# Six rotating weight blocks, wide products for a and b, and large stores on the hardware rings of ACT and SyncE, in a one-core attention-decode backward kernel

## The chip, the cores and the metric

One core of one Trainium2 chip runs the kernel. The metric is the device time of one execution in microseconds. The kernel before took 408.96 us in the median of three runs (407.39 to 410.54). Every profile shows one execution.

## What is computed

Forward and backward of a gated mix of two branches, for one token (D = 640), all in bf16: an attention decode over a cache of 4096 keys with 32 heads of 128, and a dense layer with the mish activation (F = 1728). The outputs are the mixed output and the gradients for x, K, V, wq, wo, w1, b1, w2 and the gate.

```python
q = (x @ wq).reshape(1, 1, 32, 128)
p = softmax(q . k_cache * 128**-0.5)        # 32 heads, 4096 keys each
a = (p . v_cache).reshape(1, 1, 4096) @ wo
h = x @ w1 + b1;  b = (h * tanh(softplus(h))) @ w2
g = sigmoid((x * gate_w).sum())
out = g * a + (1 - g) * b
# and the vjp of out for grad_out: dx, dK, dV, dwq, dwo, dw1, db1, dw2, dgate
```

K and V are 33.6 MB each and are read once; dK and dV have the same size and are written once. wq and wo (5.2 MB each) and w1 and w2 (2.2 MB each) are read, and as many bytes of gradients are written.

## The kernel before, in words

The 32 heads are taken in NP = 16 pairs, so the main loop has iterations i = 0 to 15, each with 16 slots s (`slot(i, s)`, L734). One pair's K or V is a tile of 128 partitions by 8192 elements (2 MB), a row of 16 KB per partition. Seven such buffers (`bufs`, tiles kv) go round. Slots 0 to 7 of iteration i transpose V of pair i for dP, slots 8 to 15 transpose K of pair i+1 for the next scores: TensorE transposes (L372), ACT copies the result out of PSUM (L375), TensorE multiplies two chunks later (L382). The softmax steps (`soft_max` to `soft_p`), `o_post`, `d_sum` and `ds_make` have fixed slots. VectorE writes dV and dK over V and K in the same buffer, in four outer products each (`outer`, L463): dV in slots 9, 10, 12 and 13, dK of the pair in slot 15 and in slots 0, 1 and 3 of the next iteration.

When a buffer's gradient is complete, `store_kv` (L725) issues its store, puts the buffer at the end of `free_q`, and `pump()` issues the next load in program order on SyncE. That load waits for the store to land. Stores are issued by GpSimd (software ring) while loads are left to issue, and by SyncE afterwards. V's store stands in slot 13, K's in slot 3 of the next iteration.

The heads fall into NG = 4 groups g of four pairs. Each group needs 1024 columns of wq (for q), a block of wo of 128 x 8 x 640 (for do, a and dwo), and leaves dwq and dwo in the same places. Before, all of wq is one resident tile `wqa`, in which w2 borrows the columns of groups 2 and 3 until dw2 is stored; wo has two buffers `wob`, group g in g mod 2. `do_sum` (L288) multiplies wo with da on VectorE, in eight rows; `dwo_row` (L353) writes dwo over wo on ACT. `dx_sum` (L484) multiplies wq with dq on VectorE, `dwq_row` (L350, in the helper `scaled`) writes dwq over wq on ACT. `mlp_dact` (L578) and `mlp_dw2` (L583) do the same with w2, `mlp_dxb` with w1, which holds buffer 4 until dw1 is stored.

What happens beside the attention is put into slots by hand: `plan(i, {s: [...]})` and `at(i, s, f, ...)` append work to slot (i, s). Each engine runs its instructions in this order; semaphores hold the dependencies. Before, wo of group g+2 is loaded one slot after group g's dwo store, into the same buffer. The work after the loop ends the last pair, and three small rows are stored by GpSimd at the end.

Of the kernel before, what the change touches and what calls it, by code (L numbers as in the profile page):

```python
# [17 lines left out]
def kernel(  # L18
# [54 lines left out]
    HC = 2 * GC  # L73
    R3 = 3 * D
# [31 lines left out]
    assert R3 <= HC and FN <= 3 * RC and FK % 3 == 1  # L106
    bufs = [big.tile([P, bufw.get(i, KVW)], BF16, name=f"kv{i}", tag=f"kv{i}") for i in range(NBUF)]
    wqa = big.tile([P, RC, H * Dh], BF16, name="wq", tag="wq")
    wob = [big.tile([P, 8, D], BF16, name=f"wo{i}", tag=f"wo{i}") for i in range(2)]
# [26 lines left out]
    def ld_w1():  # L136
# [4 lines left out]

    w2_pieces = ((wqa[:, 0:RC - 1, HC:HC + R3],
                  lambda v: v[0:FM, :].rearrange("(p k) n -> p (k n)", k=FK)[:, 0:(FK - 1) * D].rearrange(
                      "p (f x) -> p f x", x=R3)),
                 (wqa[:, RC - 1, HC:HC + D],
                  lambda v: v[0:FM, :].rearrange("(p k) n -> p (k n)", k=FK)[:, (FK - 1) * D:FK * D]),
                 (wqa[0:FR, RC - 1, HC + D:HC + 2 * D], lambda v: v[FM:F, :]))

# [4 lines left out]
    def ld_wq(c0, c1, eng=nc.sync):  # L153
        eng.dma_start(wqa[:, :, c0:c1], wq_v[:, :, c0:c1])

    def ld_wo(g):
        nc.sync.dma_start(wob[g % 2][:], wo_v[g])

    loads.append(ld_kv(kbuf, 0, Kv[0], 2, lambda: (ld_wq(0, GC), ld_wo(0))))
    loads.append(ld_kv(vbuf, 0, Vv[0], 1))  # L160
    loads.append((False, ld_w2))
    for i in range(1, NP):
        if i == 3:
            loads.append((False, lambda: ld_wq(GC, HC)))
            loads.append((False, lambda: ld_wo(1)))
        loads.append(ld_kv(kbuf, i, Kv[i], 1))
        loads.append(ld_kv(vbuf, i, Vv[i], 1))
        if i == 1:
            loads.append((True, ld_w1))
# [102 lines left out]
    def q_half(g, a, bank=misc):  # L272
        ps = bank([P, 2, 2, P], F32, "q_ps")
        for rc in range(RC):
            nc.tensor.matmul(ps[:].rearrange("p a h d -> p (a h d)"), lhsT=xc[:, rc:rc + 1].to_broadcast([P, P]),
                             rhs=wqa[:, rc, g * GC + a * 512:g * GC + (a + 1) * 512], start=(rc == 0), stop=(rc == RC - 1))
        for hh in range(2):
            h = slice(64 * hh, 64 * hh + 64)
            nc.scalar.copy(Qr[g % 2][h, 2 * a:2 * a + 2, :], ps[h, :, hh, :])
# [7 lines left out]
    def do_sum(g, k):  # L287
        nc.vector.scalar_tensor_tensor(junk[:], in0=wob[g % 2][:, k, :], scalar=1.0, in1=da_bc[:],  # L288
                                       op0=ALU.mult, op1=ALU.mult, accum_out=do8[g % 2][:, k:k + 1])
# [41 lines left out]
    def a_cols(g, c0=0, c1=RC):  # L331
        if c0 == 0:
            mst["a"] = misc([P, RC], F32, "a_ps")
        ps = mst["a"]
        wv = wob[g % 2][:].rearrange("p k (n c) -> p k c n", c=RC)
        for c in range(c0, c1):
            for k in range(8):
                nc.tensor.matmul(ps[:, c:c + 1], lhsT=wv[:, k, c, :], rhs=o8[:, k:k + 1],  # L338
                                 start=(k == 0), stop=(k == 7))
        if c1 == RC:  # L340
            if g == 0:
                nc.vector.tensor_copy(a_acc[:], ps[:])
            else:
                nc.vector.tensor_tensor(a_acc[:], a_acc[:], ps[:], ALU.add)
# [7 lines left out]
    def dwo_row(g, k):  # L352
        nc.scalar.mul(wob[g % 2][:, k, :], da_bc[:], o8f[:, k:k + 1])  # L353

    def st_dwo(g, eng, k0=0, k1=8):
        eng.dma_start(dwo_v[g][:, k0:k1], wob[g % 2][:, k0:k1])
# [125 lines left out]
    def dx_sum(g, part, c0, c1, rc):  # L482
        w = wqa[:, rc, g * GC + c0:g * GC + c1]
        nc.vector.scalar_tensor_tensor(w, in0=w, scalar=1.0, in1=dqrow[g % 2][:, c0:c1], op0=ALU.mult, op1=ALU.mult,  # L484
                                       accum_out=dq_acc[:, rc, part:part + 1])

    def dwq_row(g, c0, c1, rc, eng=nc.scalar):
        scaled(eng, wqa[:, rc, g * GC + c0:g * GC + c1], dqrow[g % 2][:, c0:c1], xf[:, rc:rc + 1])

    def st_dwq(c0, c1, eng):  # L490
        eng.dma_start(dwq_v[:, :, c0:c1], wqa[:, :, c0:c1])
# [74 lines left out]
    def mlp_b(c0, c1):  # L566
        if c0 == 0:
            mst["b"] = misc([P, RC], F32, "b_ps")
        for c in range(c0, c1):
            for k in range(FN):  # L570
                n, ks = frange(k)
                nc.tensor.matmul(mst["b"][:, c:c + 1], lhsT=w2row(k).rearrange("p (n c) -> p c n", c=RC)[:, c, :], rhs=act_b[0:n, ks], start=(k == 0), stop=(k == FN - 1))
        if c1 == RC:
            nc.vector.tensor_copy(b_acc[:], mst["b"][:])
# [6 lines left out]
    def mlp_dw2(k):  # L581
        n, ks = frange(k)
        nc.scalar.mul(w2row(k), db_bc[0:n, :], act_f[0:n, ks])  # L583

    def st_dw2():
        for t, v in w2_pieces:
            nc.gpsimd.dma_start(v(out_8), t)
# [21 lines left out]
    def st_dw1():  # L609
        nc.gpsimd.dma_start(dw1_v, bufs[mbuf["w1"]][:, 0:RC * F])  # L610
        free_q.append(mbuf["w1"])
        pump()
# [42 lines left out]
    for k in range(FN):  # L655
        at(*((2, 3), (2, 4), (2, 6), (2, 7), (2, 9), (2, 10), (2, 12), (2, 13), (2, 14), (3, 1), (3, 2), (3, 3), (3, 4),
             (3, 6))[k], mlp_dw2, k)
# [5 lines left out]
    plan(3, {9: [(st_dw2,)]})  # L663
    plan(4, {0: [(dh_row, 1)], 1: [(o_rows, 0)]})
    plan(4, {3: [(a_cols, 0, 0, 2)], 4: [(a_cols, 0, 2, 4)], 5: [(a_cols, 0, 4, 5)]})
    for k in range(8):
        at(4, (6, 7, 8, 9, 10, 12, 13, 14)[k], dwo_row, 0, k)
    plan(4, {5: rows(mlp_dxb, 0), 7: rows(mlp_dxb, 1), 14: rows(mlp_dxb, 2)})
    plan(5, {0: [(st_dwo, 0, nc.gpsimd)], 1: [(ld_wo, 2)], 5: rows(mlp_dxb, 3), 7: rows(mlp_dxb, 4), 14: dx(0, 0, 0, GC, 0)})
    plan(4, {10: [(ld_wq, HC, 2 * HC, nc.scalar)]})  # L670
    plan(6, {0: [(st_dw1,)]})

    for g in range(NG - 1):
        i = 4 * g + 4
        if g:
# [4 lines left out]
            plan(i + 1, {0: [(st_dwo, g, nc.gpsimd)]})  # L680
            if g + 2 < NG:
                plan(i + 1, {1: [(ld_wo, g + 2)]})
# [11 lines left out]
    plan(12, {8: [(st_dwq, 0, HC, nc.scalar)]})  # L694
    plan(14, {6: [(st_dwq, HC, HC + GC, nc.gpsimd)]})
# [6 lines left out]
    at(i + 1, 3, st_dwq, g * GC, g * GC + CA, nc.gpsimd)  # L702
# [31 lines left out]
    def slot(i, s):  # L734
# [16 lines left out]
        if chain_on:  # L751
            if s == 0:
                dq_row(i - 1)
            if s in (0, 1, 3):
                dk_quarter(i - 1, (0, 1, 3).index(s) + 1)
            if s == 3:
                store_kv(kbuf, i - 1, dKv[i - 1], nc.gpsimd if loads else nc.sync)
            if s == 2:
                soft_max(i)
            if s == 4:  # L760
                soft_maxt(i)
            if s == 7:
                soft_z(i)
# [9 lines left out]
        if s in (9, 10, 12, 13):  # L773
            outer(vbuf[i], st[i]["p"], Dr[(i // 4) % 2][:, i % 4, :], (9, 10, 12, 13).index(s))
            if s == 13:
                store_kv(vbuf, i, dVv[i], nc.gpsimd if loads else nc.sync)
# [118 lines left out]
    st_dwq(g * GC + CA, (g + 1) * GC, nc.gpsimd)  # L895
# [61 lines left out]
```

## Time and profile before

| | before |
|---|---|
| median of 3 runs | 408.96 us |
| span of the profiled execution | 405.7 us |
| bytes moved by DMA, mean rate | 164.88 MB, 406 GB/s |
| busy: PE / PEld / DVE / ACT / POOL | 299.9 / 275.3 / 279.1 / 259.9 / 25.1 us |
| DVE waiting for wo at L288 | 32.5 us in two waits, the longest 20.2 us |
| stores of K and V: issue to landing, median | 19.1 us (GpSimd, 25 stores), 25.5 us (SyncE, 5 whole stores) |
| loads of K and V: issue to landing, median | 18.9 us and 18.8 us |
| mean granted TensorE clock | 0.878 |

The profiled execution lasted 405.7 us from its first to its last instruction, 3.3 us less than the median of the runs. Times within it are counted from its start. PE is TensorE's matmuls, PEld its weight loads, DVE is VectorE, POOL is GpSimd, SP is SyncE. "Busy" leaves out DMA issues of the sequencers. A line such as "DVE junk L288 <- DMA wo: 32.5, 2, 20.2" reads: VectorE, at line 288, waited for the DMA that fills wo, 32.5 us in all, in 2 waits, the longest 20.2 us. In the tables by stage each engine's busy us and instruction count are followed by the granted clock, the mean busy share of the 16 DMA engines, and GB/s.

### The profile page before, as it was taken

The numbers are of one execution on the slowest core, as the hardware profiler recorded it, in microseconds if no ns is written. First come the engines' busy times: TensorE is split into PE (matmuls) and PEld (weight loads), VectorE is DVE, ScalarE is ACT, GpSimd is POOL, SyncE is SP. The second block draws the span as 40 slices with busy tenths as digits, with TensorE's granted clock in tenths as the row PEclk, the third lists the DMA queues.
The fourth block names the chain that finished last, engine by engine and source line by source line (L and its number), as shares of the span: only waits on it lengthen the run. The fifth ranks groups of instructions, "written<-read, shape, count | busy, mean of one in ns | idle before, by whom it ended". The sixth has DMA issues, their size and how long they took to land.

```text
span 405.7 us, 13024 instructions
## 1 busy us (share of the span) xinstructions
PE 299.9 (74%) x5646; PEld 275.3 (68%) x5646; DVE 279.1 (69%) x596; ACT 259.9 (64%) x529; POOL 25.1 (6%) x50
## 2 busy tenths in 40 slices
PE   3769898998886887739979869704989998896210
PEld 3548898886775777729869769603889888886200
DVE  2744969489884968529795939306889598795850
ACT  3444545699857978617768976404676998986610
POOL 3000000002000101000000100000101010000020
PEclk9886999699999889857999999955999999999555
DMA  8999999999999999999999999999999999999993
GB/s 272 425 407 436 420 421 422 425 407 361 395 427 428 412 426 425 423 430 428 430 425 428 424 429 426 427 434 429 371 401 375 386 424 424 419 422 423 426 423 124
DMA packets 15963, 164.88 MB, mean 406 GB/s; under 512 B 1713, under 2 KB 1905, under 8 KB 6178
## 3 DMA queue, kind: packets, MB, share of 16 engines
q1 hardware_dynamic: 8832, 94.08, 55.9%
q0 software_dynamic: 5472, 63.42, 37.5%
q10 hardware_dynamic: 1602, 6.56, 4.0%
q8 instruction: 44, 0.72, 0.7%
q14 instruction: 13, 0.11, 0.1%
HBM read 82.03 MB, written 82.03 MB: 404 GB/s over the span
## 4 chain that ended last, share of the span: by engine, by line
issue 44%; DMA 22%; PE 13%; DVE 9%; ACT 4%; POOL 3%; SPq 0%; POOLq 0%; ACTq 0%; DVEq 0%
DMA kv<-in_A_k_cache_dram 11%; DMA out_dram<-wo 6%; DVE kv L463 5%; PE tr L372 5%; DMA wo<-in_A_wo_dram 5%; POOL out_dram L727 2%; ACT tch L375 2%; PE dq L431 2%; PE o L431 1%; PE dP L382 1%; PE S L382 1%; DVE wq L484 1%; ACT wq L350 1%; PE a_ps L338 1%; ACT wo L353 1%
## 5 line engine op out<-in xcount | busy, mean ns | idle before, releaser
L372 PE MATMUL tr<-idf,kv 128*128 128x128 f32 x1024 | 175.3, 298 | 13.6 <-DMA kv<-in_A_k_cache_dram 11.9
L375 ACT COPY tch<-tr 128x512 f32<-128x512 f32 x256 | 144.2, 586 | 57.1 <-PE tr L372 53.2
L372 PEld LDWEIGHTS tr<-idf,kv 128*128 128x128 f32 x1024 | 120.8, 153 | 19.7 <-issue 16.7
L382 PEld LDWEIGHTS <-tch 128*128 128x128 bf16 x2048 | 89.9, 100 | 57.4 <-ACT tch L375 52.5
L463 DVE TENSOR_TENSOR kv<-p_dup,Dr 128x2048 bf16<-128x2048 bf16 x64 | 76.6, 1220 | 5.5 <-ACT p_dup L422 5.2
L463 DVE TENSOR_TENSOR kv<-ds_dup,Qr 128x2048 bf16<-128x2048 bf16 x64 | 76.8, 1220 | 0.4
L382 PE MATMUL S<-qR,tch 128*128 128x48 bf16 x1024 | 48.4, 187 | 33.5 <-ACT tch L375 32.8
L431 PEld LDWEIGHTS <-kv 128*128 128x128 bf16 x2048 | 59.2, 97 | 4.6 <-issue 3.5
L382 PE MATMUL dP<-dR,tch 128*128 128x48 bf16 x1024 | 48.7, 187 | 10.6 <-ACT tch L375 10.0
L288 DVE SCALAR_TENSOR_TENSOR junk<-wo,da_bc 128x640 bf16<-128x640 bf16 x32 | 26.3, 822 | 33.2 <-DMA wo<-in_A_wo_dram 32.5
L431 PE MATMUL dq<-ds_m,kv 128*128 128x48 bf16 x1024 | 31.8, 184 | 4.1 <-DVE ds_m L453 2.5
L422 ACT ACTIVATE p_dup<-e_m,rz 64x128 bf16<-64x128 bf16 x32 | 12.7, 397 | 33.9 <-DVE rz L416 33.4
L727 POOL DMA_DIRECT2D out_dram<-kv x25 | 13.4, 536 | 296.5 <-DVE kv L463 244.4
L431 PE MATMUL o<-e_m,kv 128*128 128x48 bf16 x1024 | 31.6, 185 | 0.0
L353 ACT ACTIVATE wo<-da_bc,o8f 128x640 bf16<-128x640 bf16 x32 | 25.9, 826 | 1.6 <-PE a_ps L338 0.9
L350 ACT ACTIVATE wq<-dqrow,xf 128x1024 bf16<-128x1024 bf16 (+2 forms) x30 | 25.1, 860 | 1.4 <-DVE wq L484 1.0
L484 DVE SCALAR_TENSOR_TENSOR wq<-wq,dqrow 128x1024 bf16<-128x1024 bf16 (+2 forms) x30 | 25.1, 862 | 0.2
L437 DVE TENSOR_TENSOR o<-o,rz 128x2 f32<-128x2 f32 x16 | 2.5, 158 | 20.6 <-PE o L431 20.6
L404 DVE TENSOR_REDUCE negM<-mt 64x1 f32<-64x64 f32 x32 | 7.1, 222 | 11.4 <-PE mt L401 10.8
L457 ACT COPY ds_dup<-ds_m 64x128 bf16<-64x128 bf16 x32 | 9.5, 297 | 6.8 <-DVE ds_m L453 6.3
L409 ACT ACTIVATE e_m<-S,negM 64x64 bf16<-64x64 f32 x32 | 10.6, 331 | 4.5 <-DVE negM L404 4.0
L578 DVE SCALAR_TENSOR_TENSOR junk<-wq,db_bc 128x640 bf16<-128x640 bf16 (+1 forms) x14 | 11.5, 820 | 2.2 <-ACT db_bc L256 1.9
(159 smaller groups left out, 240.7 us busy)
## 6 DMA issues: line engine op xcount, KB each, us to landing
out_dram<-kv POOLq DMA_DIRECT2D x25, 2048.0 KB, 19.1
kv<-in_A_v_cache_dram SPq DMA_DIRECT2D x16, 2048.0 KB, 18.8
kv<-in_A_k_cache_dram SPq DMA_DIRECT2D x15, 2048.0 KB, 18.9
out_dram<-kv SPq DMA_DIRECT2D x5, 2048.0 KB, 25.5
wo<-in_A_wo_dram SPq DMA_DIRECT2D x4, 1280.0 KB, 19.8
out_dram<-kv SPq DMA_DIRECT2D x4, 1024.0 KB, 18.5
out_dram<-wo POOLq DMA_DIRECT2D x3, 1280.0 KB, 26.2
wq<-in_A_wq_dram SPq DMA_DIRECT2D x2, 1280.0 KB, 9.4
```

The costliest lines, as they stand in the source:

```text
L288: nc.vector.scalar_tensor_tensor(junk[:], in0=wob[g % 2][:, k, :], scalar=1.0, in1=da_bc[:], op0=ALU.mult, op1=ALU.mult, accum_out=do8[g % ...
L350: nc.scalar.mul(dst, src, col)
L353: nc.scalar.mul(wob[g % 2][:, k, :], da_bc[:], o8f[:, k:k + 1])
L372: nc.tensor.transpose(tp[:, t, :], src[:, 4 * c + t, :], idf[:])
L375: nc.scalar.copy(dst[:].rearrange("p a b e -> p (a b e)").bitcast(F32), tp[:].rearrange("p a b -> p (a b)"))
L382: nc.tensor.matmul(ps[:, 4 * B:4 * B + W].rearrange("p (a b) -> p a b", b=4), lhsT=src[:, t, :, e], rhs=col[:, e, :, :].rearrange("p a b - ...
L422: nc.scalar.activation(p[HS[hh]], e_m[i % 2][HS[hh], :, hh].unsqueeze(2).to_broadcast([64, J, 2]), ACT.Copy, scale=st[i]["rz"][HS[hh], hh: ...
L431: nc.tensor.matmul(st[i][key][:].rearrange("p (a b) -> p a b", b=2), lhsT=src[:, j, :], rhs=rhs[:, j, :].unsqueeze(1).to_broadcast([P, W / ...
L463: nc.vector.tensor_tensor(kview(b)[:, j0:j0 + n, :].rearrange("p j (a b) -> p j a b", b=2), col[:, j0:j0 + n, :].unsqueeze(2).to_broadcast ...
L484: nc.vector.scalar_tensor_tensor(w, in0=w, scalar=1.0, in1=dqrow[g % 2][:, c0:c1], op0=ALU.mult, op1=ALU.mult, accum_out=dq_acc[:, rc, par ...
L578: nc.vector.scalar_tensor_tensor(junk[0:n, :], in0=w2row(k), scalar=1.0, in1=db_bc[0:n, :], op0=ALU.mult, op1=ALU.mult, accum_out=dact[0:n ...
L727: eng.dma_start(dst, bufs[b][:, 0:J * Dh])
```

## The change

- **Six rotating blocks.** `wqa` and `wob` become six blocks `wblk` of 128 x 5120. Group g's wq lies in block 0, 4, 2, 0, its wo in block 1, 5, 3, 1; w2 lies in blocks 2 and 3, until dw2 is stored. wq is loaded by groups (1280 KB each, row pieces of 2 KB), wo and wq of group 2 in (5,1), wo 3 in (8,4), wq 3 in (9,4).
- **Issuers.** Stores of K and V, dw1, dw2 and dwo go from GpSimd to ACT, dwq (by group) to SyncE, its last part to ACT. GpSimd keeps the small inputs at the start and the three result rows.
- **Slots.** V's store moves from (i,13) to (i+1,0), K's from (i+1,3) to (i+1,5); dw2's store from (3,9) to (3,15), dwo 0's from (5,0) to (7,0), and dwo 0's rows from iteration 4 to 5 and 6.
- **dw2's rows**: six of fourteen go from ACT to VectorE, the rest are spread out.
- **Wide products**: the products for a and b have 48 columns (the last operand repeated) instead of 1, and a column step of 1 overwrites the surplus.

```diff
-    wqa = big.tile([P, RC, H * Dh], BF16, name="wq", tag="wq")
-    wob = [big.tile([P, 8, D], BF16, name=f"wo{i}", tag=f"wo{i}") for i in range(2)]
+    wblk = [big.tile([P, RC * GC], BF16, name=f"wb{i}", tag=f"wb{i}") for i in range(6)]
+    WQB, WOB, W2B = (0, 4, 2, 0), (1, 5, 3, 1), (2, 3)
+    wqt = [wblk[b][:].rearrange("p (r c) -> p r c", r=RC) for b in WQB]
+    wot = [wblk[b][:].rearrange("p (k n) -> p k n", k=8) for b in WOB]
...
+    w2_pieces = ((wblk[W2B[0]][:], lambda v: w2_main(v)[:, 0:8 * D]),
+                 (wblk[W2B[1]][:, 0:(FK - 8) * D], lambda v: w2_main(v)[:, 8 * D:FK * D]),
+                 (wblk[W2B[1]][0:FR, (FK - 8) * D:(FN - 8) * D], lambda v: v[FM:F, :]))
...
     def a_cols(g, c0=0, c1=RC):
         if c0 == 0:
-            mst["a"] = misc([P, RC], F32, "a_ps")
+            mst["a"] = misc([P, RC + W], F32, "a_ps")
...
-                nc.tensor.matmul(ps[:, c:c + 1], lhsT=wv[:, k, c, :], rhs=o8[:, k:k + 1],
+                nc.tensor.matmul(mst["a"][:, c:c + W], lhsT=wv[:, k, c, :], rhs=o8[:, k:k + 1].to_broadcast([P, W]),
...
-    def mlp_dw2(k):
+    def mlp_dw2(k, eng=nc.scalar):
         n, ks = frange(k)
-        nc.scalar.mul(w2row(k), db_bc[0:n, :], act_f[0:n, ks])
+        scaled(eng, w2row(k), db_bc[0:n, :], act_f[0:n, ks])
     def st_dw2():
         for t, v in w2_pieces:
-            nc.gpsimd.dma_start(v(out_8), t)
+            nc.scalar.dma_start(v(out_8), t)
...
     def st_dw1():
-        nc.gpsimd.dma_start(dw1_v, bufs[mbuf["w1"]][:, 0:RC * F])
+        nc.scalar.dma_start(dw1_v, bufs[mbuf["w1"]][:, 0:RC * F])
...
-    for k in range(FN):
-        at(*((2, 3), (2, 4), (2, 6), (2, 7), (2, 9), (2, 10), (2, 12), (2, 13), (2, 14), (3, 1), (3, 2), (3, 3), (3, 4),
-             (3, 6))[k], mlp_dw2, k)
+    for k in range(6):
+        at(2, 3 + k // 3, mlp_dw2, k, nc.vector)
+    for k, (i, s) in enumerate(((2, 7), (2, 10), (2, 13), (3, 3), (3, 6), (3, 9), (3, 12), (3, 14))):
+        at(i, s, mlp_dw2, 6 + k)
...
-    plan(3, {9: [(st_dw2,)]})
+    plan(3, {15: [(st_dw2,)]})
...
-    for k in range(8):
-        at(4, (6, 7, 8, 9, 10, 12, 13, 14)[k], dwo_row, 0, k)
+    for k, (i, s) in enumerate(((5, 5), (5, 9), (5, 10), (5, 12), (6, 9), (6, 10), (6, 12), (6, 13))):
+        at(i, s, dwo_row, 0, k)
...
-    plan(5, {0: [(st_dwo, 0, nc.gpsimd)], 1: [(ld_wo, 2)], ...})
-    plan(4, {10: [(ld_wq, HC, 2 * HC, nc.scalar)]})
+    plan(5, {1: [(ld_wo, 2), (ld_wq, 2)], ...})
+    plan(7, {0: [(st_dwo, 0, nc.scalar)]})
+    plan(8, {1: [(st_dwq, 0, 0, GC, nc.sync)], 4: [(ld_wo, 3)]})
+    plan(9, {4: [(ld_wq, 3)]})
...
-            plan(i + 1, {0: [(st_dwo, g, nc.gpsimd)]})
-            if g + 2 < NG:
-                plan(i + 1, {1: [(ld_wo, g + 2)]})
+            plan(i + 1, {0: [(st_dwo, g, nc.scalar)]})
...
-    plan(12, {8: [(st_dwq, 0, HC, nc.scalar)]})
-    plan(14, {6: [(st_dwq, HC, HC + GC, nc.gpsimd)]})
+    plan(11, {1: [(st_dwq, 1, 0, GC, nc.sync)]})
+    plan(14, {6: [(st_dwq, 2, 0, GC, nc.sync)]})
...
-    at(i + 1, 3, st_dwq, g * GC, g * GC + CA, nc.gpsimd)
+    at(i + 1, 3, st_dwq, g, 0, CA, nc.sync)
...
         if chain_on:
             if s == 0:
                 dq_row(i - 1)
+                store_kv(vbuf, i - 1, dVv[i - 1], nc.scalar if loads else nc.sync)
             if s in (0, 1, 3):
                 dk_quarter(i - 1, (0, 1, 3).index(s) + 1)
-            if s == 3:
-                store_kv(kbuf, i - 1, dKv[i - 1], nc.gpsimd if loads else nc.sync)
+            if s == 5:
+                store_kv(kbuf, i - 1, dKv[i - 1], nc.scalar if loads else nc.sync)
...
-            if s == 13:
-                store_kv(vbuf, i, dVv[i], nc.gpsimd if loads else nc.sync)
...
-    st_dwq(g * GC + CA, (g + 1) * GC, nc.gpsimd)
+    st_dwq(g, CA, GC, nc.scalar)
```

## Prediction

> **What bounds the kernel now.** I read the DMA queues first, since the third part of the page has a kind and a share for each ring. The columns are packets, megabytes, and the time the packets took as a share of all 16 DMA engines over the span.
>
> ```profile
> q1 hardware_dynamic: 8832, 94.08, 55.9%
> q0 software_dynamic: 5472, 63.42, 37.5%
> q10 hardware_dynamic: 1602, 6.56, 4.0%
> HBM read 82.03 MB, written 82.03 MB: 404 GB/s over the span
> ```
>
> q1 is SyncE's ring, q10 ACT's, q0 GpSimd's. With 0.8% of small kinds the shares add up to 98.2%: the 16 engines have almost no free time. Then the table by stage: busy us of PE, PEld, DVE, ACT and POOL with instruction counts, the granted clock, the DMA share, GB/s.
>
> ```profile
> 90.00:110.00 20.00, 16.53 (x328) 14.54 (x324) 18.26 (x39) 18.39 (x39) 2.93 (x5) 1.00 0.96 371
> 180.00:260.00 80.00, 67.93 (x1323) 63.19 (x1324) 61.43 (x117) 59.67 (x123) 4.79 (x9) 0.94 1.01 427
> 280.00:320.00 40.00, 37.70 (x717) 35.01 (x713) 31.91 (x66) 28.92 (x64) 2.13 (x4) 0.93 0.97 381
> 169.00:182.00 13.00, 4.94 (x64) 4.35 (x60) 1.99 (x4) 1.61 (x5) 0.00 (x0) 0.53 1.01 431
> 258.00:279.00 21.00, 3.10 (x73) 2.76 (x69) 1.84 (x4) 1.71 (x4) 0.00 (x0) 0.68 1.00 428
> 398.00:405.70 7.70, 0.00 (x0) 0.00 (x0) 0.00 (x0) 0.00 (x0) 0.00 (x0) 0.50 0.11 45
> ```
>
> 427 GB/s is the saturated rate. From 169 to 182 and from 258 to 279 all compute stands still and the DMA runs on at 428 to 431: compute has about 33 us in hand and the transfers set the time. Only two stretches after the start fall short: 90 to 110 (371) and 280 to 320 (381). The last row is the fixed end. The waits name the two stalls:
>
> ```profile
> DVE junk L288 <- DMA wo<-in_A_wo_dram: 32.5, 2, 20.2
> SPq L131 <- DMA out_dram<-kv: 275.1, 25, 22.8
> SPq L157 <- DMA out_dram<-wo: 12.3, 2, 7.8
> ```
>
> DVE stands twice at do_sum (L288) for a wo block; the third line says why it is late: with two wo buffers, the load (L157) has to wait until that buffer's dwo store has landed. The second line is normal traffic: each K or V load waits for its buffer's store. After the second stall no finished K or V buffers were there to store, and the transfers ran dry: SyncE's timeline has loads at 286.34, 299.84 and 310.05 us, each alone behind one store.
>
> **The change, part by part.** Bytes stay: 164.88 MB. So I price what changes in the time the DMA engines need, and in the time they stand dry.
>
> *The late stretch.* With six blocks, wo and wq of group 2 go where w2 was, and are issued in iteration 5, slot 1, after a dw2 store of iteration 3, slot 15: 18 slots, some 26 us, apart. wo of group 3 is issued at (8,4), 20 slots behind its dwo store at (7,0). Before, load and store stood one slot apart. L288's 32.5 us vanish, and no drained pipeline follows. The shortfall is (427 - 381) x 40 us = 1.84 MB, at 427 GB/s 4.3 us. I take all of it: -4.3. Bounds: -4.3 to 0, if the dry time moves elsewhere. The compute stalls themselves gain nothing; the transfers cover them.
>
> *Smaller packets.* In the trace's packet records 16,384 bytes take 612 ns, 4,096 take 162, 2,048 between 86 (50 to 70 us) and 102 (the start), 1,280 take 61; for 1,024 I estimate 49, from the last two slopes. The hardware rings make one packet of each row piece, GpSimd's ring puts 4,096 bytes together. dwq goes from 1,280 packets of 4,096 (208 us of engine time) to 1,920 of 2,048 and 1,280 of 1,024 (165 + 63 = 228). wq's loads go from 1,280 of 2,048 and 640 of 4,096 (214) to 2,560 of 2,048 (220). w2 saves 5, having rows of 10,240 and 6,400 bytes instead of 3,840. Net 21 us over 16 engines: +1.3, with 102 ns for every 2,048 it is near +4; near the saturated rows I take +1.1 (0 to +4).
>
> *Later stores in the early phase.* The V store moves from slot 13 to slot 0 of the next iteration, the K store from 3 to 5. Copy times at L375 give the slots: V stores were issued at 67.4 and 91.2, and (2,0) and (3,0) lie at 70.8 and 94.9; K stores at 77.3 and 98.0, with (2,5) and (3,5) at 80.2 and 101.3. So each comes 3 to 4 us later where compute sets the pace, and dw2's 2.2 MB come 11 us later (99.7 to about 111) and no longer fill this gap. Against it, ACT, 18.39 of 20 us busy at 90 to 110, is rid of work:
>
> ```profile
> L583 ACT ACTIVATE wq<-db_bc,act_f 128x640 bf16<-128x640 bf16 (+1 forms) x14 | 11.8, 844 | 0.2
> L353 ACT ACTIVATE wo<-da_bc,o8f 128x640 bf16<-128x640 bf16 x32 | 25.9, 826 | 1.6 <-PE a_ps L338 0.9
> ```
>
> Six of 14 dw2 rows go to DVE (6 x 0.844 = 5.1 us off ACT in iteration 2), eight dwo rows leave iteration 4 (6.6 us). On DVE a row costs at most the 0.82 of the same shape at L578; DVE was idle for 5.2 of the 10 us from 70 to 80, which hides three of them, and the rest delay one softmax by about 1 us. Compute then runs some 2.5 us earlier by (3,0). I follow the transfers by hand from 60 to 115 us and find about 3 us dry, against (427 - 371) x 20 / 427 = 2.6 now: +0.4. Bounds -2.6 (never dry) to +8 (four gaps of 2 us).
>
> *Who issues.* Thirty-one DMAs come to ACT. Its own row:
>
> ```profile
> 132.14 0.83 ACT L353 ACTIVATE wo<-da_bc,o8f 128x640 bf16<-128x640 bf16 x1
> 132.28 0.67 ACTq L154 DMA_DIRECT2D wq<-in_A_wq_dram  x1
> 132.88 0.57 ACT L375 COPY tch<-tr 128x512 f32<-128x512 f32 x1
> ```
>
> The issue (0.67 us) lies under the running activation; the next copy starts on time. Price 0, at worst 31 x 0.35 to 0.67, 11 to 21 us of ACT, within compute's 33. The store's wait for DVE is covered too: at (i+1,0) ACT has already waited in dq_row for a DVE cast behind the last outer product, and at (i+1,5) in soft_exp for negM, behind dk_quarter 3. Behind the store in ACT's queue stand the copies that feed PE, so this cover matters. dwq on SyncE waits for ACT rows finished one slot earlier, while SyncE lags by a store's landing; behind it stand K and V loads, 8 us late at worst, with 32 slots between issue and use.
>
> *The ring itself.* From 190 to 230 us 16,384-byte packets took 618 ns on the software ring and 612 on the hardware one. If all of q0's 37.5% x 405.7 us shrank by that 1%, it would be -1.5; from 120 to 280 the two are equal (616, 615), which says 0. I take -0.8. The Trainium skill, DMA: Bandwidth & Descriptors, section Issuing engines are not separate DMA queues, says that all three issuers end on the same 16 engines and only the sequencer's issue time is saved; the equal packets agree. By it this term is 0 and the sum below 402.9.
>
> *Wide a and b products.* 230 matmuls go from 1 to 48 columns: L338 shows 178 ns, L431 184 at 48, 1.4 us of PE in all, under compute's slack. 0.
>
> **Sum**: 405.7 - 4.3 + 1.1 + 0.4 - 0.8 = 402.1 us of span. The profiled execution's span lies 3.3 below the median of 408.96; the same distance gives 405.4.
>
> **Rivals.**
>
> *Never dry.* If compute, freed from ACT rows, keeps stores coming, the early 2.6 goes as well: 405.7 - 4.3 - 2.6 + 1.1 - 0.8 = 399.1, median 402.4. For it: ACT's 9.9 of 10 us at 90 to 100. Against: stores come later by design, dw2 too.
>
> *The dry time only moves.* Compute arrives early, but loads hang behind 2,048-byte packets on SyncE's ring, or stores come in bunches. Then only +1.1 and +0.4 remain: 407.2, median 410.5. For it: from 51 to 62 us wq's small packets alternated with 16,384-byte ones, and took 13 us for 1.3 MB. Against: the engines were busy all the while.
>
> *ACT held by shared completion slots (slower).* In the built order of the changed kernel every hardware-ring DMA waits for the one issued eight before it; the rings of SyncE and ACT share the eight. Before, the stores had GpSimd's own eight. Eight of ACT's issues now stand behind a load or a SyncE store: the db1 row at (4,0) behind K5's load, K stores at (5,5), (6,5), (7,5), (8,5), (9,5), (11,5), (12,5) behind loads of K6, wo 2, K8, V9, the dwq 0 store, and loads of K12 and K13. ACT then feeds PE nothing until that transfer has landed. Loads land 18.9 us after issue (median), and SyncE issues late, so each can stand 0 to 10 us. Most come three slots before the data are needed anyway. It decides beyond the 33 us of slack plus the 7.6 between compute's end (390.8) and the last transfer (398.4). At 6 us each, 48 us, compute ends 48 - 33 - 7.6 = 7 later than the transfers do now, and stalls drain them: 405.7 + 7 + 1.1 = 413.8, median 417. Against: while ACT stands, other loads (two to four) are queued, so the engines stay busy; at 3 us each it costs nothing.
>
> **How the numbers follow.** Forecast 0.48 (405.4, its own range 403 to 408), never dry 0.15, moved 0.16, ACT held 0.21. About 1%, 404.9 and 413.0, is what a measurement of this kernel can tell from no change. The forecast's middle lies just inside: 0.23 of it faster, 0.25 the same. Faster 0.23 + 0.15 = 0.38, same 0.25 + 0.16 + 0.01 = 0.42, slower 0.20. Range 401 to 413: it takes in never dry and moved, and the mild end of ACT held; the packet and early bounds fit inside.
>
> **What would show it.** Right: no wait at do_sum for wo above 3 us, 425 GB/s or more from 280 to 320, about 371 at 90 to 110, 16,384-byte packets at 612 to 616 ns, DMA shares adding up to about 98%, the last transfer near 395. Wrong: ACT idle before a store for a load to land, for more than 30 us in all; copies at L375 late behind it; new dry stretches; a span under 399 or over 408.

## The result, and the profile after

The changed kernel took 415.38 us in the median of four runs (414.06 to 416.56), the kernel before 408.7 beside it: a ratio of 1.0161, 95% interval 1.0122 to 1.02. It is 6.7 us slower. I had forecast 405.4, with a range up to 413: wrong in sign and outside the range. The profiled execution's span is 412.1 us (before 405.7). The ratios, here and below, leave out executions in a slower state, of which e1, e2, e6 and e10 had one each; the medians include them.

The DMA queues first (packets, megabytes, share of the 16 engines over the span):

```profile
q1 hardware_dynamic: 12384, 101.29, 61.2%
q10 hardware_dynamic: 5490, 62.76, 36.1%
q0 software_dynamic: 256, 0.01, 0.1%
HBM read 82.03 MB, written 82.03 MB: 398 GB/s over the span
```

The same bytes and again 98.2% of the engines' time, with the 0.8% of small kinds. So the engines did not stand idle for a larger share of the time: the same bytes took them longer. The table by stage shows where (columns as in the prediction; the last two are DMA share and GB/s). Before:

```profile
70.00:80.00 10.00, 9.88 (x133) 9.34 (x133) 4.79 (x11) 5.19 (x12) 0.53 (x1) 0.66 0.99 423
110.00:120.00 10.00, 8.07 (x169) 7.25 (x168) 8.43 (x16) 6.22 (x15) 0.57 (x1) 1.00 1.01 429
150.00:170.00 20.00, 15.04 (x325) 14.08 (x323) 14.80 (x25) 16.81 (x31) 1.59 (x3) 1.00 1.00 423
310.00:330.00 20.00, 18.34 (x390) 17.11 (x389) 14.77 (x28) 18.20 (x36) 1.60 (x3) 1.00 1.00 389
```

After:

```profile
70.00:80.00 10.00, 9.21 (x160) 8.81 (x159) 6.22 (x15) 4.57 (x11) 0.00 (x0) 1.00 0.99 370
110.00:120.00 10.00, 7.17 (x133) 6.58 (x132) 6.35 (x9) 5.42 (x13) 0.00 (x0) 0.84 0.97 367
150.00:170.00 20.00, 15.97 (x330) 14.25 (x327) 17.08 (x29) 18.73 (x34) 0.00 (x0) 1.00 1.00 384
181.00:192.00 11.00, 0.82 (x4) 0.85 (x5) 2.06 (x2) 0.63 (x2) 0.00 (x0) 0.67 1.00 428
280.00:320.00 40.00, 27.28 (x493) 24.32 (x491) 26.09 (x52) 19.31 (x43) 0.00 (x0) 0.87 0.99 407
310.00:330.00 20.00, 17.99 (x389) 17.46 (x388) 14.14 (x30) 15.14 (x33) 0.00 (x0) 1.00 0.95 369
```

At 427 GB/s the shortfalls of the first three stretches against before are 10 x 53 / 427 = 1.2, 10 x 62 / 427 = 1.5 and 20 x 39 / 427 = 1.8 us. The stretch from 280 to 320 gained 26 GB/s (2.4 us; before 381, in the prediction), but 310 to 330 fell from 389 to 369. Counted in bytes moved since the start, at 427 GB/s, the changed kernel is 4.0 us behind the kernel before at 170 us, 5.1 at 280, 2.7 at 320, 3.7 at 330 and 5.3 at 390. The share column is what misleads: 384 GB/s at a share of 1.00 means that packets take longer for their bytes. I added the durations of all packets in the trace's packet records and divided by 16: 398.1 us before, 404.4 after. The rest of the span is 7.6 and 7.8 us. So 6.3 of the 6.4 us of span are packet time. It splits into the 16,384-byte packets on SyncE's ring (3,968 of loads and 640 of the last stores of K and V; mean 625 before, 646 ns after; their excess over 612 ns is 3.7 us before, 9.7 after; of it 3.6 and 9.4 are the loads'), those of the other stores (626 and 618 ns; excess 2.9 and 1.2) and packets of 1,000 to 4,096 bytes, whose time beyond the rate of the large ones is 3.0 and 4.5 us: +6.0 - 1.7 + 1.5 = +5.8.

The waits on compute's side (us in all, times, longest):

```profile
PE tr L372 <- DMA kv<-in_A_v_cache_dram: 10.5, 2, 10.3
PE q_ps L275 <- DMA wb<-in_A_wq_dram: 10.1, 2, 9.3
ACT tch L375 <- DMA kv<-in_A_v_cache_dram: 5.2, 1, 5.2
ACT tch L375 <- DMA kv<-in_A_k_cache_dram: 5.2, 1, 5.2
SPq L154 <- DMA out_dram<-wb: 11.6, 1, 11.6
```

VectorE's waits for wo at do_sum are gone, as forecast (L288 stands idle for 0.7 us). In their place TensorE waits for V of pair 7 at 181 us and for wq of group 3 at 286 us. The chain that ended last passes through the same transfers (start, us, what):

```profile
159.85 31.20 DMA kv<-in_A_v_cache_dram
233.79 29.93 DMA out_dram<-wb
263.73 32.30 DMA wb<-in_A_wq_dram
```

V7's load stands on SyncE's ring behind wo 2 and wq 2 (issued at 155.0 and 156.5) and lands 31 us after issue. dwq 0's store landed 29.9 us after its issue; only then could wq 3's load start, and it took 32.3 us. The DMA issues give the medians (KB each, us to landing):

```profile
out_dram<-kv ACTq DMA_DIRECT2D x25, 2048.0 KB, 14.3
wb<-in_A_wq_dram SPq DMA_DIRECT2D x4, 1280.0 KB, 29.2
wb<-in_A_wo_dram SPq DMA_DIRECT2D x4, 1280.0 KB, 12.3
```

The same 1280 KB take 12.3 us as wo and 29.2 as wq. wq's packets are 2,048 bytes long: from 264 to 296 us, while wq 3 lands, the records have 640 of them and 743 of 16,384 bytes, so that the short ones get few of the bytes. The row pieces aren't all of it: wq of group 0, at the start, took 9.3 us, and in the kernel before, wo's four loads in long pieces took 11.8 to 41.8.

### The profile page after: what moved, and what is told of

The parts are those of the page before. It is cut to its first block, busy times and chain, and to the rows that moved or that the text cites. A ratio compares the mean times of both kernels' runs of the same rounds, so it can differ in the third digit from the quotient of the medians.

```text
span 412.1 us, 12990 instructions
## 1 busy us (share of the span) xinstructions
PE 303.6 (74%) x5643; PEld 276.1 (67%) x5646; DVE 280.7 (68%) x602; ACT 256.4 (62%) x523; POOL 5.1 (1%) x15
## 4 chain that ended last, share of the span: by engine, by line
PE 32%; DMA 29%; DVE 23%; ACT 9%; issue 4%; POOL 0%; ACTq 0%; POOLq 0%; SPq 0%; DVEq 0%
DVE kv L463 12%; PE tr L372 12%; DMA wb<-in_A_wq_dram 10%; DMA kv<-in_A_v_cache_dram 8%; DMA out_dram<-wb 7%; ACT tch L375 3%; PE dP L382 3%; PE o L431 3%; PE q_ps L275 3%; DMA out_dram<-kv 3%; PE S L382 2%; PE dq L431 2%; DVE junk L288 2%; DVE wb L484 2%; DMA kv<-in_A_k_cache_dram 2%
## 5 line engine op out<-in xcount | busy, mean ns | idle before, releaser
L382 PE MATMUL dP<-dR,tch 128*128 128x48 bf16 x1024 | 49.7, 189 | 21.4 <-ACT tch L375 19.8
L353 ACT ACTIVATE wb<-da_bc,o8f 128x640 bf16<-128x640 bf16 x32 | 25.9, 826 | 1.6 <-PE a_ps L338 1.0
L288 DVE SCALAR_TENSOR_TENSOR junk<-wb,da_bc 128x640 bf16<-128x640 bf16 x32 | 26.3, 821 | 0.7
L350 ACT ACTIVATE wb<-dqrow,xf 128x1024 bf16<-128x1024 bf16 (+2 forms) x30 | 24.9, 859 | 1.2 <-DVE wb L484 0.8
L484 DVE SCALAR_TENSOR_TENSOR wb<-wb,dqrow 128x1024 bf16<-128x1024 bf16 (+2 forms) x30 | 25.1, 863 | 0.2
L275 PE MATMUL q_ps<-wb,xc 128*128 128x512 bf16 x37 | 12.2, 459 | 10.5 <-DMA wb<-in_A_wq_dram 10.1
L396 DVE TENSOR_REDUCE m<-S 64x1 f32<-64x64 f32 x32 | 7.0, 219 | 14.6 <-PE S L382 14.4
L279 ACT CAST Qr<-q_ps 64x256 bf16<-64x256 f32 x16 | 5.9, 366 | 17.5 <-PE q_ps L275 17.4
L275 PEld LDWEIGHTS <-xc 128*128 128x128 bf16 x40 | 4.7, 121 | 15.3 <-issue 13.3
## 6 DMA issues: line engine op xcount, KB each, us to landing
wb<-in_A_wq_dram SPq DMA_DIRECT2D x4, 1280.0 KB, 29.2
wb<-in_A_wo_dram SPq DMA_DIRECT2D x4, 1280.0 KB, 12.3
```

What stands on the lines that cost most here:

```text
L288: nc.vector.scalar_tensor_tensor(junk[:], in0=wot[g][:, k, :], scalar=1.0, in1=da_bc[:], op0=ALU.mult, op1=ALU.mult, accum_out=do8[g % 2][ ...
L350: nc.scalar.mul(dst, src, col)
L353: nc.scalar.mul(wot[g][:, k, :], da_bc[:], o8f[:, k:k + 1])
L382: nc.tensor.matmul(ps[:, 4 * B:4 * B + W].rearrange("p (a b) -> p a b", b=4), lhsT=src[:, t, :, e], rhs=col[:, e, :, :].rearrange("p a b - ...
```

## The experiments

Eighteen kernels. Ratios are to the kernel before, run beside them (medians 407.8 to 408.3 us). "Packets" is the time of all packets over 16 engines, "rest" the profiled span less that, "excess" that of the 16,384-byte packets on SyncE's ring, most of them loads', over 612 ns, in us. These three are of one execution each, up to 3 us from the median (e17's took 413.4 us, e8's 409.2).

| kernel | median | ratio (95%) | packets | rest | excess |
|---|---|---|---|---|---|
| before | 408.7 | | 398.1 | 7.6 | 3.7 |
| changed | 415.38 | 1.0161 (1.0122, 1.02) | 404.4 | 7.8 | 9.7 |
| e1 changed, K/V by GpSimd | 413.86 | 1.0134 (1.0094, 1.0175) | 401.2 | 10.1 | 5.8 |
| e2 changed, K/V on ACT in old slots | 416.79 | 1.0203 (1.0147, 1.0258) | 405.8 | 10.9 | 10.0 |
| e3 changed, K/V by GpSimd, old slots | 415.49 | 1.0185 (1.0139, 1.023) | 405.1 | 8.2 | 8.7 |
| e4 before, K/V in new slots | 407.76 | 0.9997 (0.9978, 1.0015) | 397.6 | 7.7 | 4.1 |
| e5 changed, no wait for wq 3 | 414.51 | 1.0165 (1.0124, 1.0205) | 403.2 | 9.2 | 8.6 |
| e6 changed, dwq by GpSimd | 413.18 | 1.0107 (1.0066, 1.0148) | 402.0 | 8.1 | 7.6 |
| e7 e6 and e3 together | 420.75 | 1.0318 (1.0273, 1.0363) | 403.2 | 14.7 | 8.7 |
| e8 before, no wait for wo 3 | 407.85 | 0.9991 (0.997, 1.0012) | 397.5 | 9.9 | 4.7 |
| e10 changed, transfers early again | 410.84 | 1.007 (1.0042, 1.0099) | 400.6 | 6.7 | 6.0 |
| e11 before, dw2 as changed | 407.76 | 1.0002 (0.9976, 1.0027) | 398.7 | 6.6 | 4.3 |
| e12 before, wq loads as changed | 409.0 | 1.0019 (0.9996, 1.0043) | 399.2 | 7.5 | 4.7 |
| e13 before, dwq as changed | 411.52 | 1.0089 (1.0061, 1.0116) | 401.2 | 7.9 | 6.6 |
| e14 e10, dwq by GpSimd | 410.8 | 1.0058 (1.0033, 1.0082) | 399.8 | 9.4 | 5.4 |
| e15 e13, but dwq by ACT | 409.37 | 1.0019 (0.9996, 1.0043) | 398.4 | 6.7 | 4.0 |
| e16 before, issuers as changed | 410.64 | 1.0059 (1.0035, 1.0083) | 400.6 | 7.0 | 7.7 |
| e17 e11, e12 and e13 together | 416.39 | 1.0192 (1.0134, 1.0251) | 402.9 | 8.7 | 7.0 |
| e18 e14, large stores by GpSimd, K/V in old slots | 417.44 | 1.0231 (1.019, 1.0272) | 400.8 | 15.9 | 6.4 |
| e19 e17, but dwq by ACT | 413.67 | 1.0164 (1.0099, 1.023) | 403.1 | 7.0 | 7.9 |

### Who stores K and V, and when (e1 to e4)

```diff
# e1: the changed kernel
-   store_kv(vbuf, i - 1, dVv[i - 1], nc.scalar if loads else nc.sync)     # s == 0
+   store_kv(vbuf, i - 1, dVv[i - 1], nc.gpsimd if loads else nc.sync)
-   store_kv(kbuf, i - 1, dKv[i - 1], nc.scalar if loads else nc.sync)     # s == 5
+   store_kv(kbuf, i - 1, dKv[i - 1], nc.gpsimd if loads else nc.sync)
# e2: nc.scalar as changed, but V's store at (i,13) and K's at (i+1,3)
# e3: e2 with nc.gpsimd
# e4: the kernel before, V's store at (i+1,0) and K's at (i+1,5), nc.gpsimd
```

> The changed kernel, but K and V stores are issued by GpSimd (software ring, completion slots of their own) in the new, later slots; the rest as changed. Theory L (shared completion slots: ACT and SyncE wait for each other's transfers, ACT lost 16 us in three such waits): the loss goes, 404 to 408 us, and ACT has no wait of 5 us before its copies. Theory S (the later store slots make loads and stores run in turns, and loads that run alone have slow packets, 646 ns instead of 625): stays slow, 412 to 416, load packets near 646 ns. Theory W (wq's 2 KB packets on SyncE's ring hold K and V loads behind them): stays slow, 412 to 416, with the stalls at (7,0) and (11,2).

> The changed kernel with K and V stores on ACT, but in the slots of before (13 and 3). Theory L: as slow as the changed kernel or slower, 413 to 418, since ACT also waits for DVE. Theory S: 405 to 409, load packets near 625 ns. Theory W: 412 to 416.

> The changed kernel with K and V stores on GpSimd and in the slots of before: only the six blocks, dw2, dwo and dwq as changed are left. Theories L and S: both their causes are gone, 402 to 407. Theory W: 410 to 416, the stalls at (7,0) and (11,2) stay.

> The kernel before with only the store slots moved (V to slot 0 of the next iteration, K to slot 5), still on GpSimd. Theory S: 411 to 416, slower by 1% or more. Theories L and W: 408 to 410, no change.

None of e1, e2 and e3 gives back more than a fifth of the loss (1.0134 in e1 against 1.0161, the intervals overlap), and the late slots on the kernel before cost nothing (e4). So theory L falls with e1 and e3, theory S with e2, e3 and e4; theory W is near the times of all four. ACT held by completion slots, my slower rival, is in the changed kernel's trace (the two ACT waits above and one of 5.6 us at the same line), but e1 takes K's and V's stores off ACT and stays slow. So it isn't what sets the time.

### The stall for group 3's weights (e5, e8), and dwq's issuer (e6, e7)

```diff
# e5: the changed kernel; q of group 3 is computed from group 1's wq block
-   rhs=wqt[g][:, rc, a * 512:(a + 1) * 512]
+   rhs=wqt[1 if g == 3 else g][:, rc, a * 512:(a + 1) * 512]
# e8: the kernel before; do_sum of group 3 reads wo 2's buffer
-   in0=wob[g % 2][:, k, :]
+   in0=wob[0 if g == 3 else g % 2][:, k, :]
# e6: the changed kernel; dwq of groups 0 to 2 and 3's first half
-   (st_dwq, 0, 0, GC, nc.sync)        # and the others alike
+   (st_dwq, 0, 0, GC, nc.gpsimd)
# e7: e6, with K's and V's stores as in e3
```

> The changed kernel, but q of group 3 is made with the block of wq 1 instead of wq 3 (so q of group 3 is that of other weights); every load and store stays. Only TensorE's wait at (11,2) for wq 3 is taken away. Theory C (the chain dwq 0 store, wq 3 load, q, then compute to the end sets the time): the 12 us stall goes, and the time falls by 6 to 12 us, to 403 to 409. Theory F (the DMA engines' own time, 404.4 us of packets before and after any stall, sets it): 413 to 417, no change.

> The changed kernel with dwq 0, 1, 2 and the first part of dwq 3 stored by GpSimd, in the same slots; K and V stores stay on ACT. Theory C: dwq 0 is issued near 218 us instead of 233.8, its packets are 4,096 bytes and no K or V load queues behind it, so wq 3 lands some 15 to 20 us earlier: 404 to 409. Theory F: the larger packets save about 1 us, 411 to 415.

> As the run before, and K and V stores by GpSimd in the slots of before as well: the six blocks and their loads remain, the large stores are mostly back on the software ring. Theory C: 402 to 408. Theory F: 409 to 414. If 2 KB wq loads on SyncE's ring are a cause of their own, the stall at (7,0) for V7 stays at 8 to 12 us.

> The kernel before, but do_sum of group 3 reads the buffer of wo 2 instead of wo 3 (so that group's do is that of other weights); every load and store stays. Only VectorE's 20 us wait for wo 3 is taken away. Theory C (before was paced from 277 us on by that load and the compute behind it): 397 to 403. The view of the prediction (the DMA engines set the time, a stall costs only the 4.3 us that they stand dry after it): 404 to 406.

e8 bears most on my forecast. It removes the stall of 20 us that my largest term rested on, and gains nothing that can be told: 0.9991, where the view of the prediction wanted 404 to 406 us. Its stretch from 280 to 320 us, and the wait that grew, before and in e8:

```profile
280.00:320.00 40.00, 30.07 (x617) 28.67 (x617) 24.71 (x52) 23.79 (x51) 1.60 (x3) 0.87 1.00 420
```

```profile
PE tr L372 <- DMA kv<-in_A_k_cache_dram: 11.9, 4, 5.9
```

```profile
PE tr L372 <- DMA kv<-in_A_k_cache_dram: 26.0, 9, 8.1
```

The transfers do recover: 420 GB/s against 381, or 40 x 39 / 427 = 3.7 of the 4.3 us that I had priced. But compute runs ahead to K loads it has to wait for (10.8 us between the copies of slots 7 and 8 of iteration 11), the last K load is waited for until 354.3 us, and while compute ends the last pair, from 390 to 400 us, the transfers run at 279 GB/s, before at 353. The time without packets grows from 7.6 to 9.9 us. e5 does the same to the changed kernel's wait for wq 3: the wait is gone (10.1 to 0.7 us), and 280 to 320 us carries the 425 GB/s that I had wanted:

```profile
280.00:320.00 40.00, 28.44 (x539) 26.24 (x536) 28.07 (x54) 20.41 (x46) 0.00 (x0) 0.87 1.01 425
```

The time stays (1.0165), and TensorE's waits for K grow in its place (5.9 to 19.2 us). So neither of these two stalls sets its kernel's time. e6 is 0.5% faster than the changed kernel, some 2 us, but the intervals overlap. e7 lies outside the ranges of both its theories. It is 2.1% slower than e6, with the rest of the span at 14.7 us, and 1.3% slower than e3, from which it differs in dwq's issuer alone. So dwq by GpSimd costs time where GpSimd also stores K and V (e7 against e3), and none that can be told where ACT does (e6).

### The moved transfers, together and singly (e10 to e13)

```diff
# e10: the changed kernel; dw2 rows and store as before, and
-   for k, (i, s) in enumerate(((5, 5), (5, 9), ...)): at(i, s, dwo_row, 0, k)
+   for k in range(8): at(4, (6, 7, 8, 9, 10, 12, 13, 14)[k], dwo_row, 0, k)
-   plan(5, {1: [(ld_wo, 2), (ld_wq, 2)], ...})
+   plan(4, {10: [(ld_wq, 2, nc.scalar), (ld_wo, 2, nc.scalar)]})
+   plan(5, {0: [(st_dwo, 0, nc.scalar)], ...})
-   plan(7, {0: [(st_dwo, 0, nc.scalar)]})
# e11: the kernel before; dw2's rows and store as in the change, by GpSimd
# e12: the kernel before
-   plan(4, {10: [(ld_wq, HC, 2 * HC, nc.scalar)]})
+   plan(5, {1: [(ld_wo, 2), (ld_wq, HC, HC + GC)], ...})
+   plan(9, {4: [(ld_wq, HC + GC, 2 * HC)]})
# e13: the kernel before
-   plan(12, {8: [(st_dwq, 0, HC, nc.scalar)]})
-   plan(14, {6: [(st_dwq, HC, HC + GC, nc.gpsimd)]})
+   plan(8, {1: [(st_dwq, 0, GC, nc.sync)]})
+   plan(11, {1: [(st_dwq, GC, HC, nc.sync)]})
+   plan(14, {6: [(st_dwq, HC, HC + GC, nc.sync)]})
```

> The changed kernel with group 0's and w2's transfers back in the slots before: dw2 rows on ACT in iterations 2 and 3 with the store at (3,9), dwo 0 rows in iteration 4 with the store at (5,0), and wo 2 and wq 2 loaded together (2.56 MB) from ACT at (4,10), as large and as early as the wq load that stood there. Blocks, rings, dwq by group and the K and V stores' slots stay as changed. Theory M (the transfers moved out of 100 to 180 us had kept loads and stores mixed; without them the loads run alone, and their packets take longer): the time falls to 409 to 411.5, the excess of 16,384-byte load packets over 612 ns falls from 9.7 us to under 6, and the slices from 110 to 170 us carry 410 GB/s or more. Theory P (the blocks' small row pieces, wq and dwq by group on SyncE's ring, cost it wherever the others stand): it stays at 414 to 416.

> The kernel before with only dw2 as changed: six rows on DVE at (2,3) and (2,4), eight on ACT in other slots, the store at (3,15) instead of (3,9), still by GpSimd. Theory M with dw2 as its largest part: 2 to 4 us slower (410 to 412), with a dip below 380 GB/s near 100 to 115 us. Theory M with the loads of wq as its largest part: within 1 us (407 to 409). Theory P: within 1 us.

> The kernel before with only the load of wq for groups 2 and 3 as changed: instead of 2.56 MB from ACT at (4,10), group 2's 1.28 MB on SyncE's ring at (5,1) behind wo 2, and group 3's at (9,4). Theory M: 3 to 6 us slower (411 to 414), with compute held for wq 2 or for V7 near 180 us and slices below 400 GB/s between 130 and 170 us. Theory P: 1 to 3 us slower, by the 2,048-byte pieces in place of 4,096, with no dip from 130 to 170.

> The kernel before with only the dwq stores as changed: group by group in 2,048-byte pieces from SyncE at (8,1), (11,1) and (14,6), and group 3's first half from SyncE, instead of groups 0 and 1 together from ACT at (12,8) and the rest by GpSimd. Theory P: 3 to 6 us slower (411 to 414), K and V loads behind them late. Theory M: at most 2 us slower (408 to 410), since nothing of it leaves the stretch from 100 to 180 us.

e10 gives back 0.9%, some 3.7 us, more than half, as theory M had it. Its stretches, as in the table above:

```profile
110.00:120.00 10.00, 8.06 (x148) 7.21 (x147) 6.51 (x11) 5.01 (x12) 0.00 (x0) 0.89 1.01 430
150.00:170.00 20.00, 15.07 (x323) 14.02 (x323) 16.33 (x30) 16.43 (x33) 0.00 (x0) 1.00 1.01 428
181.00:192.00 11.00, 8.29 (x138) 7.02 (x135) 7.27 (x12) 5.64 (x12) 0.00 (x0) 1.00 1.00 425
280.00:320.00 40.00, 28.94 (x509) 25.71 (x508) 23.83 (x51) 19.90 (x48) 0.00 (x0) 0.87 0.99 397
```

The dips at 110 and 150 us are filled, and compute no longer stands from 181 to 192. From 110 to 120 us the changed kernel moved 3.5 MB of loads and 0.1 of stores, e10 2.9 and 1.4, and loads' 16,384-byte packets took 612 ns instead of 696. From 150 to 170 the changed kernel had 4.8 MB of loads, 1.2 of them in wq's 2,048-byte packets, beside 2.9 of stores; e10 has 2.1 beside 6.5, and 619 ns instead of 677. The part after 280 us is not repaired. e10 also takes wo 2 and wq 2 out of SyncE's queue, where V7 stood behind them, so it doesn't part the place of a transfer from its queue. Of the single edits, dw2's slot costs nothing, wq's late loads 0.8 us (not told from zero by the interval), less than either theory wanted, and dwq by group on SyncE 3.4 us.

### Ring or packet size, ring alone, and sums (e14 to e17)

```diff
# e14: e10, with every st_dwq by nc.gpsimd
# e15: e13, with nc.scalar for nc.sync in the four st_dwq
# e16: the kernel before
-   nc.gpsimd.dma_start(v(out_8), t)     # likewise dw1 and dwo 0 to 2
+   nc.scalar.dma_start(v(out_8), t)
    # K and V: nc.scalar, V at (i+1,0), K at (i+1,5)
# e17: the kernel before with the edits of e11, e12 and e13
```

> The changed kernel with the early transfers of e10 (410.8) and dwq's stores by GpSimd in place of SyncE and, at the end, ACT. Theory Q (two causes that add: the moved transfers, some 4.5 us, and dwq on SyncE's ring, some 2 to 3.5 us): 407 to 409, no difference from before. Theory O (one cause with two cures; whatever evens out the transfers gives it back): as e10, 410 to 412.

> The kernel before with dwq by group in the changed slots as in e13 (411.5), but issued by ACT, so the packets are 2,048 bytes as in e13 and SyncE's ring holds loads alone, as before. Theory R (what cost 3.4 us in e13 is SyncE's ring: each dwq store waits there for its rows, with K and V loads behind it): 407.5 to 409.5, with K loads no later at (10,7) than before. Theory P (the 2,048-byte packets, or the slots): 411 to 412.

> The kernel before with only the stores' issuer changed: K and V stores from ACT in the changed slots, dw2, dw1 and dwo from ACT; the blocks, the weights' slots and dwq (its last three stores by GpSimd) as before. My prediction's terms for it, -0.8 for the ring and at most +0.4 for the later stores: 407 to 409. A rival, that ACT waiting for a completion slot or a late store costs part of what is left unexplained: 410 to 413.

> The kernel before with the three single edits of e11 (dw2 late: no difference), e12 (wq loads late: +0.8 us) and e13 (dwq by group on SyncE: +3.4 us) together, rings and wo blocks as before. If they add: 412 to 413. Theory M (each alone is made up by the others, since something else fills the gap; together nothing does): 414 to 417.

e15 against e13 is the cleanest pair. The same 2,048-byte packets in the same slots cost 0.9% from SyncE and 0.19% from ACT, which the interval does not tell from zero: it was SyncE's queue, not the packets. ACT issued dwq 0's store at 211.0 us, SyncE only at 230.8. In both chains wo 3's load stands late; in e13's:

```profile
254.71 30.77 DMA wo<-in_A_wo_dram
```

and in e15's:

```profile
262.52 15.03 DMA wo<-in_A_wo_dram
```

e13's load is issued earlier and lands later, behind dwq 0's store and K and V loads on the same queue. After the stall that follows (29.4 us between the copies of slots 7 and 8 of iteration 10, against 20.7 before) the transfers ran at 346 and 351 GB/s for two slices.

e16 puts a number to the rings, with the late slots that cost nothing in e4: +0.59%, 2.4 us, where I had summed -0.4. Its stretches:

```profile
70.00:80.00 10.00, 8.89 (x122) 8.52 (x122) 5.19 (x8) 3.42 (x7) 0.00 (x0) 0.66 0.97 352
280.00:320.00 40.00, 36.51 (x686) 33.93 (x687) 32.81 (x67) 28.64 (x64) 0.00 (x0) 0.90 0.94 370
```

The first of them ran at 423 GB/s before. ACT does wait for completion slots there too (9.2 us in two waits), but what grew is packet time, 398.1 to 400.6 us, with the excess on SyncE's ring from 3.7 to 7.7 and the other stores' from 2.9 to 1.0. The packet records show a change that goes with it. Between 70 and 130 us, 82% of before's 16,384-byte load packets start in a microsecond in which such a packet of a store starts as well; in e16 it is 21%, in the changed kernel 23%. Loads and stores take turns there: in the four 10 us from 70 to 110 us e16 has 168, 43, 212 and 28 of the loads' 16,384-byte packets, and 46, 210, 27 and 227 of the stores'. All seven profiles with K's and V's stores on ACT's ring show 21 to 34%; of thirteen with GpSimd's, eleven show 46 to 96%, and e13 and e18 30 and 36%. That a load packet is slow because it runs alone doesn't follow: in the changed kernel those alone took 725 ns and those beside stores 638, but in e16 686 and 694, and in the kernel before 612 and 640.

e17: the three edits cost 1.9% together, and 1.1% as the sum of the single ratios; so a loss as large as the change's can be made on the kernel before with the transfers of the weights and their gradients alone. e14: dwq by GpSimd gives nothing that can be told on top of e10.

### Blocks without rings, and e17 without SyncE's dwq (e18, e19)

```diff
# e18: e14, with nc.gpsimd for dw1, dw2, dwo 0 to 2, K and V, V at (i,13), K at (i+1,3)
# e19: e17, with nc.scalar for nc.sync in the four st_dwq
```

> The changed kernel's six blocks and wide products alone: group 0's and w2's transfers early as in e10, all large stores by GpSimd, K and V in the slots before. wq in 2,048-byte pieces group by group, wo 3 and wq 3 on SyncE's ring at (8,4) and (9,4) stay. Theory Q (the ring costs about 2.4 us, as in e16, and the moved transfers the rest; the blocks themselves nothing): 407 to 409. Theory O (what is left in e14, 2.4 us, is the blocks' own, wq by group among the loads and the wait for wq 3): 410 to 412.

> The kernel before with the three edits of e17 (416.4), but dwq by group issued by ACT as in e15, so that SyncE's ring carries loads alone. Theory R (wq's late loads and dwq's stores cost so much together because both stand in SyncE's one queue ahead of K and V): 408.5 to 411. Theory M (the late wq loads and dw2 need nothing of dwq to cost it): 413 to 417.

e18 met neither theory: 417.4, a ratio 1.7% above that of e14, from which it differs in the stores' issuers and K's and V's slots alone. Its chain and one of its waits:

```profile
239.76 29.81 DMA out_dram<-kv
270.09 35.10 DMA wb<-in_A_wq_dram
```

```profile
PE q_ps L275 <- DMA wb<-in_A_wq_dram: 23.5, 2, 22.3
```

A K store lands 29.8 us after its issue by GpSimd, 3 us behind dwo 1's in the same queue. A K load waits for it on SyncE, and wq 3's load behind that takes 35.1 us. q waits 22 us, and after this stall two slices run at 219 and 303 GB/s. So the 2.4 us left in e14 can't be booked to the rings by subtraction: with blocks, issuers and slots as changed save 1.7% against all large stores in GpSimd's one queue in the old slots, with the old layout they cost 0.6%. No run with blocks parts the issuers from the slots there. e19 is 1.6% slower, as theory M had it, its interval overlaps e17's, and its three edits singly (e11, e12, e15) sum to 0.4%: they reinforce one another even with dwq off SyncE's queue.

No version tried beats the kernel before; e4, e8, e11, e12 and e15 can't be told from it.

## Why the prediction was wrong, step by step

- **"The late stretch: -4.3."** The mechanism was seen rightly up to the wait: six blocks took L288's wait away. The step that failed is "I take all of it". e8 takes the longer of the two stalls out of the kernel before: 280 to 320 us recovers 3.7 us, as I had it, and the run gains 0.4 us, with an interval that includes zero. What I took for time won, compute gives back at the next late loads (26.0 us of waits for K instead of 11.9) and at the end of the last pair. In the changed kernel, too, this stretch recovers 2.4 us, and the run is slower. My own bound of 0, "if the dry time moves elsewhere", was the right value. "Dry" was misread as well: in my own row the engines' share is 0.97, so at most 1.2 of the 4.3 us were idle engines, and the 16,384-byte packets there took 662 to 669 ns instead of 612.
- **"Bytes stay. So I price what changes in the time the DMA engines need, and in the time they stand dry."** The failing premise, and the largest miss that one run measures: I priced no term for transfers that change place. The 2.56 MB of wq that ACT issued at 132 us, and dwo 0's and dw2's stores, were moved out of 100 to 145 us. e10 puts the stores back, with wo 2 and wq 2 in wq's place, and gains 3.7 us. And "dry" was the wrong measure here too: the new dips have a DMA share of 0.95 to 1.00.
- **"dwq on SyncE ... 8 us late at worst, with 32 slots between issue and use"**, priced at nothing. dwq 0's store itself took 29.9 us to land, wq 3's load depends on it, and both queue among K and V loads. e13 measures 0.9% for this edit, e15 0.19% with ACT as issuer. For wo 3 I had counted the slots between store and load; for wq 3 ((8,1) to (9,4), needed at (11,2)) I did not set the 32 us of a load in 2,048-byte packets against them, though my rival named 13 us for 1.3 MB at the start.
- **"The ring itself: -0.8"** and **"later stores: +0.4"**. The stores' packets did get faster, by 1.7 us rather than 0.8, and later slots alone cost nothing (e4, e11). But loads' packets got slower by more: in e16 the run lost 2.4 us. I priced one direction's packets without asking what the other direction does when the stores' timing changes. The Trainium skill, DMA: Bandwidth & Descriptors, section Issuing engines are not separate DMA queues, which I weighed there, would have given 0 for the issuer. The runs don't agree: e13 and e15 differ by 0.7% through the issuer alone, with dwq 0's store issued at 230.8 us by SyncE and at 211.0 by ACT.
- **"Smaller packets: +1.1"** was about right: +1.5 us in the packet records. 2,048 bytes took 89.9 ns in the mean (I had used 86), 1,024 bytes 46 to 47 (I had estimated 49, where the slopes I named give 52). The upper bound, by its own figures, was 4.5 rather than 4. GpSimd's ring joined two row pieces to a packet, 2,048 to 4,096 bytes, but also dw2's 3,840 to 7,680, so that 4,096 is not a fixed size there.
- **Wide products at 0, dw2's rows on DVE hidden**: nothing contradicts it. A dw2 row took 0.38 us on DVE (bound 0.82), a product at L338 204 ns instead of 178, and e11 is 1.0002. No run has the wide products alone.
- **The rivals.** "The dry time only moves" came nearest to what the traces show, loads behind 2,048-byte packets and stores in bunches, and had 410.5 us as its price, since it gave the moved dips nothing beyond what was lost before. "ACT held" had the right side and nearly the size (417) by luck: e1 takes K's and V's stores off ACT, and the time stays.
- **What would show it**: L288's wait went and the shares add up to 98%, as said, but neither told right from wrong. 280 to 320 ran at 407 instead of 425, 90 to 110 at 389 instead of about 371, and 16,384-byte packets on SyncE's ring took 646 ns. The last transfer landed at 411.1 us, 6.8 later than before instead of 3 earlier; before it was 404.3, not the 398.4 that I had read.

**What stays open.** Why the parts reinforce each other (e17, e19) and why issuers and slots as changed cost 0.6% with the old layout and save 1.7% with blocks is told by the traces only as queues of late loads. The excess on SyncE's ring parts the kernels in two (all with 4.7 us or less lie within 0.2% of before, all with 5.4 or more are 0.5% or more slower), but among the slower ones it doesn't give the order (e18 has 6.4 at 1.0231, the changed kernel 9.7 at 1.0161). No run changed the taking of turns by itself, so that it is the cause isn't shown. The move of dwo 0 alone was not tried.

## What to carry to other kernels

When the DMA engines are the bound, don't price a stall of compute, or the slow stretch behind it, as time to be won until you have asked where compute waits next: in e5 and e8 the stall was gone, the stretch ran at full rate, and the time stayed. Price instead every transfer that changes its place: what it filled, what now stands behind it on its issuer's queue, and how long a load in short packets takes beside long ones, against the slots until its use. And read GB/s beside the DMA share: a share of 1.00 at 384 GB/s is lost time too.

## What the runs showed of the hardware

- In the changed kernel, loads of 1280 KB in 2,048-byte packets took 26 to 33 us beside transfers of 16,384-byte packets, the same bytes in long row pieces 11.6 to 13.0; in the kernel before, long row pieces took up to 41.8.
- Loads' 16,384-byte packets, mostly 612 ns long, took 696 in the mean from 110 to 120 us of the changed kernel, with the engines' share at 0.97 and 367 GB/s; in e10, with the stores of dw2 beside them, 612 at 1.01 and 430.
- With K's and V's stores on ACT's hardware ring, loads and stores took turns from 70 to 130 us in all seven profiles (21 to 34% of load packets beside a store's); with GpSimd's ring nearly so in two of thirteen (30 and 36%).
- The same four dwq stores cost 0.9% from SyncE, in one queue with the loads of K and V, and from ACT nothing that can be told (e13, e15).
